# Global queries' scores for four head pairs in one pass of small pieces, the softmax division moved ahead of the values, and a new fixed order

## The chip, the cores and the metric

The kernel runs on one core of a Trainium2 chip. The metric is the device time of one execution in microseconds (us), as the median of several runs; lower is better. A core has five engines that run their own instruction streams and wait for each other by semaphores: TensorE (PE, matmuls), VectorE (DVE), ScalarE (ACT), GpSimd (POOL) and SyncE (SP, which here issues all DMAs).

## The reference

Attention with 32 global and 512 local tokens per head (8 batches, 8 heads, 64 numbers a head), then a gated product with two weight pairs. All inputs of the attention are float32, the weights float64; the output is float32.

```python
k_all, v_all = concat([k_g, k_l]), concat([v_g, v_l])
out_g = softmax(scale * q_g @ k_all.T) @ v_all            # 32 global queries see all 544 keys
s_ll  = where(abs(i - j) <= 32, scale * q_l @ k_l.T, -1e9) # local queries: a band
out_l = softmax(concat([scale * q_l @ k_g.T, s_ll])) @ concat([v_g, v_l])
x = concat([out_g, out_l]).transpose(...).reshape(8 * 544, 512)
out = ((x @ w1) * (x @ w2)) @ w3 @ w_out                   # 512 -> 1024 -> 1024 -> 512
```

Each softmax divides by its sum plus 1e-9.

## The kernel before

The work goes by pairs of heads, 32 pairs, four to a batch. Heads of a pair lie on partitions 0 to 63 and 64 to 127.

**A local pair.** Keys (tile `kr`, 128 x 544) and queries are loaded, keys are spread into `KT` so that each block of 32 queries finds its 128 keys in one stretch. `scores` (L412) makes 32 small float32 matmuls, each with 64 rows and 32 columns of weights and 128 moving columns, into the PSUM tile `s`. `minus_max` (L417, DVE) adds the mask and takes the minimum, `exps` (L423, ACT) makes the exponentials in place in `P` and their sums, `inverse` (L427, L428) the reciprocals. `turn` (L449, L452, DVE) transposes `P` by blocks into `TT` and `PT`, eight `move` steps (L466, L464) bring the blocks that belong to neighbours to their partitions, on whichever engine the plan names. `values` (L477 to L489) makes the products with the values into PSUM tile `av`, for the local queries and, from `TGr` and `TGg`, for the global ones. DVE and ACT add the two halves into `u`. The division by the sums is made here: `inverse_out` stores the reciprocals to DRAM (`rd`), `inverse_in` loads them spread over 64 partitions (`R`), and `normalize` (L444) multiplies `u` in two halves. `convert` splits `u` into a high and a low part (tiles `x`) for the gated product. From pair 5 on, `values` of a pair and `scores` of the next stand together on PE.

**Global queries.** In batch 0, `g_scores` (L523) multiplies a pair's keys by `QG`, in which the two heads' queries stand on the diagonal, in float32, 128 rows and 512 and 32 columns. In later batches keys are split into `kph` and `kpl` (`prep_kp`), queries into a high and a low half of `QG` (`prep_qg`), and four matmuls of the faster type float32r make the sum; ACT copies one half (`g_half`, `cg`) and DVE adds it (`g_minus_max`, L540). Two pairs share a tile `Pg`. `g_exps`, `g_normalize` follow, then, for batch 0, transposes on PE (`g_transposes`, L558), later block transposes on DVE and a trip over DRAM (`g_turn`, `g_out`, `g_in`, L576 to L589) into `TGr`.

**Weights.** Float64 words are loaded (`raw`, 512 KB each, three buffers), DVE and ACT make float32 of them (`unit`, L671 to L675). `fold` (L751) multiplies w3 by w_out on PE, eight tiles of 512 columns (`w`) with eight float32 products each, two PSUM banks. w1 and w2 (`w12`, eight numbers, four early in 512 KB pieces, four later in 256 KB pieces named `w12s`) are split into high and low parts.

**The gated product.** `first` (L617 to L619, tiles `ap`, `bp`) makes x @ w1 and x @ w2 in three float32r products, `gate_*` multiply and split, `second` (L649 to L651, `acc`) multiplies by the folded weights. It runs over two halves of each batch, four quarters a half, two w12 numbers a quarter.

**The order.** All steps are listed with what they wait for; `PLAN` holds, for every step, its place and its engine, and the program issues each engine's instructions in just this order. Each engine works strictly in its order. Tiles that are reused form rings: `pu` is the ring of two PSUM buffers (two banks each) that `s`, `av`, `sg` and `tg` share.

Of the kernel before, what the change touches and what calls it, by code (L numbers as in the profile page):

```python
# [20 lines left out]
KD, KX = 544, 832  # L21
# [6 lines left out]
def i(ap):  # L28
# [3 lines left out]
NX, NO, NK, NQ, MA = (5, 6), 3, 3, 3, 4  # L32
# [3 lines left out]
    kph=647, kpl=(726, 1374), qgh=298, qgl=(250, 461), kx=(440, 750, 1500), mmax=371, exps=500, inv=350, mul=(420, 740),  # L36
    turn=(1520, 790), move=(420, 420, 500, 560), cb=(590, 600), cu=(230, 200), sum=650, joing=500, xh=405, xl=(411, 740),
    cg=610, mg=790, eg=840, ng=820, wg=(683, 292), ga=588, gb=691, gh=620,
    gl=(691, 1295), out=587, shift=(434, 295), scale=(680, 440), merge=(676, 424), w12h=(676, 423),
    w12l=((691, 1300), (420, 752)), w34h=587, w34l=681, gscores=505,  # L40
    gtrans=465, gturn=1010, first=1372, second=1382, fold=860,
    scores=1290, values=2240, both=3110, gscores32=930,
# [3 lines left out]
FRONT = (("s", 0), ("sg", 0), ("sg", 1), ("s", 1), ("tg", 0))  # L46
# [3 lines left out]
IDLE = {None: ((0, 128, 256), (0, 64, 256), (64, 128, 256), (0, 64, 256), (64, 128, 256))}  # L50
# [12 lines left out]
    ('w3', 0, 0), ('wo', 0, 0), ('w3', 1, 0), ('wo', 1, 0), ('wo', 2, 0), ('wo', 3, 0), ('w3', 0, 1), ('wo', 4, 0),  # L63
    ('w3', 1, 1), ('wo', 5, 0), ('wo', 6, 0), ('wo', 7, 0), *[('w3', t, e) for t in range(2, 8) for e in range(2)],
    *[('w12', m, e) for m in range(MA) for e in range(2)],
)

# [3 lines left out]
    1V 632S 0V 2843V 3V 633S 8S 634D 677S 635D 329S 374S 10A 12S 636P 645D 637D 372P 638A 646A 152S 5V 647D 678S 648A  # L71
    649D 639D 16S 679A 641D 640A 643D 722S 651D 328S 642A 652A 375P 4V 9D 373D 11D 644A 376D 14A 650A 767S 20S 680A 7V
    377A 656D 681P 378D 379P 657D 380A 690D 663S 13D 682D 381D 684D 18A 692D 661A 15D 694D 660S 686D 382S 724A 696D
    687A 664V 658V 665D 659V 24S 695A 17D 662V 21D 723S 688D 683A 685A 22A 725A 383P 23D 812S 666P 689A 248P 697A 26A
    19D 691A 653D 384D 693A 6V 667A 28S 668A 25D 30A 27D 701D 702D 249P 710A 394A 669D 654S 386P 698D 726P 32S 154A
    258P 29D 2V 331S 706S 31D 703D 727D 707V 709A 735D 259P 705A 704D 387D 729D 737D 332V 334V 708V 731D 260P 769A 736A
    711P 158S 36S 34A 728A 388A 261P 250P 739D 251P 153D 732A 33D 741D 38A 35D 742A 40S 655S 37D 733D 39D 740A 730A 42A
    712A 44S 395D 389D 770A 713A 41D 333V 48S 768S 714D 43D 45D 738A 46A 335D 390P 252P 52S 47D 734A 385S 56S 391A 50A
    262P 396P 253P 747D 392A 49D 51D 397A 54A 263P 746D 670V 814A 771P 254P 671V 53D 60S 753A 264P 699S 55D 856S 748A
    780D 751V 755A 750A 674V 255P 398D 754A 749D 752V 772D 672A 64S 57D 256A 58A 773A 257D 774D 265P 59D 756P 782D 781A  # L80
    675A 62A 61D 68S 268P 63D 776D 700S 66A 269P 266D 72S 164S 70A 65D 270P 784D 400A 271P 67D 272P 778D 273P 743D 69D
    785A 267D 274P 278P 74A 275P 159D 779A 716D 279P 76S 786D 777A 71D 401D 676V 402P 280P 276D 775A 73D 75D 281P 673D
# [24 lines left out]
    1035V 899V 2120P 992P 441D 896D 978A 2131P 2132P 2127A 2133P 2134P 966S 442S 993D 1001D 979A 1003D 941D 995D 1002A
    996A 2135A 1005D 1006A 997D 999D 1007D 980D 445V 967S 939A 1004A 2128D 446D 1008A 1078V 998A 2136D 443S 994A 1000A
# [121 lines left out]
def band_attention_glu_kernel(  # L230
# [78 lines left out]
    def fresh(what, b):  # L309
# [899 lines left out]
```

## Time and profile before

| | |
|---|---|
| median of 3 runs | 772.17 us (771.96 to 774.92) |
| profiled execution: time | 772.31 us |
| profiled execution: span, first to last instruction | 770.6 us |
| mean granted TensorE clock | 0.989 |
| busy in the span: PE, DVE, ACT, POOL | 98%, 58%, 48%, 14% |
| HBM read and written | 61.57 MB, 12.94 MB |

Times are us from the start of the span. A row of the timeline has start, duration, engine, line, operation, tiles and shapes; "x8" says that eight records were merged into the row. A float32 matmul leaves two records. Matmul rows overlap, so what one costs is read from its start to the next row's start. Idle time stands in brackets with what ended it.

### The profile page before, as it was taken

To read this page: it belongs to the slowest core of one execution; us is meant where nothing else is said; L and a number is where in the kernel's file an instruction comes from. 1 tells how busy PE (TensorE), PEld (TensorE's weight loads), DVE (VectorE), ACT (ScalarE), POOL (GpSimd) and SP (SyncE) were. 2 spreads that over 40 slices of the span, in tenths; PEclk is the share of its full clock that TensorE was granted. 3 is DMA by queue.
4 is the path that set the end of the run, shared out by engine and by line. 5 is a ranking of instruction groups with operands and counts; after the bars stand their busy time and mean duration, and the time that the engine had idled before them with its cause. 6 is when DMAs were issued, how large, how long until landed. Compare 5 with 4: busy or idle time off the path is not lost.

```text
span 770.6 us, 22271 instructions
## 1 busy us (share of the span) xinstructions
PE 757.7 (98%) x9098; PEld 667.4 (87%) x9098; DVE 444.2 (58%) x1331; ACT 366.9 (48%) x1081; POOL 104.2 (14%) x194
## 2 busy tenths in 40 slices
PE   6999999999999999999999999999999999999998
PEld 4554589899999999999999999999999999999997
DVE  5889888565555647374666665665647474412121
ACT  4767777454444545354544455455446453312111
POOL 4110223434220001000001111010001001000000
PEclk7899999999999999999999999999999999999999
DMA  8887875223172313223232423241312121100000
GB/s 256 235 273 249 254 198 173 74 67 102 32 227 77 108 53 93 77 70 96 77 98 86 103 79 102 60 131 60 90 56 84 50 62 47 45 1 28 2 28 27
DMA packets 58301, 77.64 MB, mean 101 GB/s; under 512 B 19192, under 2 KB 28632, under 8 KB 58200
## 3 DMA queue, kind: packets, MB, share of 16 engines
q1 hardware_dynamic: 58200, 76.23, 33.3%
q8 instruction: 71, 1.16, 0.6%
q14 instruction: 30, 0.25, 0.1%
HBM read 61.57 MB, written 12.94 MB: 97 GB/s over the span
## 4 chain that ended last, share of the span: by engine, by line
PE 89%; DMA 4%; DVE 3%; ACT 2%; issue 1%; SPq 0%; POOL 0%; DVEq 0%; ACTq 0%
PE bp L617 8%; PE ap L617 8%; PE acc L649 8%; PE acc L651 8%; PE acc L650 8%; PE ap L618 8%; PE bp L618 8%; PE ap L619 8%; PE bp L619 8%; PE s L412 4%; PE av L477 4%; DMA raw_w<-in_w_t_dram 3%; PE sg L523 2%; PE w L751 2%; PE av L486 2%; PE av L482 2%
## 5 line engine op out<-in xcount | busy, mean ns | idle before, releaser
L617 PE MATMUL bp<-x,w12h 128*128 128x256 f32 x544 | 153.3, 282 | 0.2 <-issue 0.2
L617 PE MATMUL ap<-x,w12h 128*128 128x256 f32 x544 | 153.0, 281 | 0.3 <-ACT x L373 0.2
L618 PE MATMUL bp<-x,w12h 128*128 128x256 f32 x544 | 150.8, 277 | 0.6 <-issue 0.6
L618 PE MATMUL ap<-x,w12h 128*128 128x256 f32 x544 | 150.9, 277 | 0.2 <-DVE x L376 0.2
L619 PE MATMUL bp<-x,w12l 128*128 128x256 f32 x544 | 150.5, 277 | 0.0
L619 PE MATMUL ap<-x,w12l 128*128 128x256 f32 x544 | 150.5, 277 | 0.0
L423 ACT ACTIVATE P<-P,small 128x128 f32<-128x128 f32 x256 | 101.4, 397 | 34.5 <-DVE small L417 33.4
L417 DVE CUSTOM_DVE_ANT_0 P<-s,cs 128x128 f32<-128x128 f32 x256 | 68.0, 283 | 67.9 <-PE s L412 65.6
L617 PEld LDWEIGHTS ap<-x,w12h 128*128 128x128 f32 x544 | 102.1, 188 | 4.6 <-issue 1.6
L617 PEld LDWEIGHTS bp<-x,w12h 128*128 128x128 f32 x544 | 102.1, 188 | 4.5 <-issue 2.4
L618 PEld LDWEIGHTS bp<-x,w12h 128*128 128x128 f32 x544 | 102.4, 188 | 3.0 <-issue 1.3
L618 PEld LDWEIGHTS ap<-x,w12h 128*128 128x128 f32 x544 | 102.4, 188 | 2.5 <-DVE x L376 0.4
L619 PEld LDWEIGHTS ap<-x,w12l 128*128 128x128 f32 x544 | 102.2, 188 | 0.0
L619 PEld LDWEIGHTS bp<-x,w12l 128*128 128x128 f32 x544 | 102.2, 188 | 0.0
L751 PE MATMUL w<-wo,w3f 128*128 128x512 f32 x128 | 59.1, 609 | 0.1
L423 ACT ACTIVATION_READ_ACCUMULATOR P<-P,small 128x1 f32 x256 | 48.1, 188 | 0.0
L751 PEld LDWEIGHTS w<-wo,w3f 128*128 128x128 f32 x128 | 23.6, 193 | 26.8 <-issue 24.1
L466 ACT COPY PT<-TT 32x256 f32<-32x256 f32 (+1 forms) x101 | 39.1, 387 | 14.1 <-DVE TT L449 12.4
L373 ACT COPY u<-av 128x512 f32<-128x512 f32 (+1 forms) x40 | 19.1, 489 | 51.4 <-PE av L489 51.3
L449 DVE STREAM_TRANSPOSE TT<-P 128x1024 f32<-128x1024 f32 x32 | 38.9, 1217 | 1.9 <-ACT P L423 1.8
L412 PE MATMUL s<-KT,qp 64*32 64x128 f32 x2048 | 38.6, 281 | 1.0 <-POOL KT L318 0.6
L477 PEld LDWEIGHTS av<-PT,vr 64*64 64x64 f32 x1024 | 28.7, 135 | 10.9 <-issue 8.1
(789 smaller groups left out, 1430.9 us busy)
## 6 DMA issues: line engine op xcount, KB each, us to landing
raw_w<-in_w_t_dram SPq DMA_DIRECT2D x24, 512.0 KB, 5.8
kq<-in_kp_t_dram SPq DMA_DIRECT2D x32, 272.0 KB, 3.2
out_dram<-o_None SPq DMA_DIRECT2D x33, 256.0 KB, 2.6
qp<-in_q_t_dram SPq DMA_DIRECT2D x32, 256.0 KB, 3.2
vr<-in_v_t_dram SPq DMA_DIRECT2D x32, 256.0 KB, 3.7
R<-rd SPq DMA_DIRECT2D x64, 128.0 KB, 3.1
raw_wo<-in_wo_t_dram SPq DMA_DIRECT2D x8, 512.0 KB, 5.9
raw_w12s<-in_w_t_dram SPq DMA_DIRECT2D x16, 256.0 KB, 3.5
```

The source lines that it names most:

```text
L412: nc.tensor.matmul(st[32 * a : 32 * a + 32, x, 128 * e : 128 * e + 128], q[r, 128 * e + 32 * a : 128 * e + 32 * a + 32], k[r, o : o + 128] ...
L417: nc.vector.tensor_tensor_reduce(Ps[m % 2][:, x, e], T["s", m][:, x, 128 * e : 128 * e + 128], masks[e], -0.125, 3.0e38, ALU.add, ALU.min, ...
L423: nc.scalar.activation(p, p, AF.Exp, bias=T["mn", n][:, e : e + 1], scale=-1.0, accum_out=T["sm", m][:, x, e : e + 1])
L466: (nc.scalar.copy if eng is nc.scalar else eng.tensor_copy)(dst, src)
L477: nc.tensor.matmul(av[c, y, 128 * k + 32 * s0 : 128 * k + 32 * s1], V[r, x, k], PT[r, s0:s1, x, k], start=(k == 0), stop=False, **go)
L617: nc.tensor.matmul(d, wh[:, k, c, :], x[:, 0, 0:w], start=(k == m % 2 == 0), stop=False, skip_group_check=True)
L618: nc.tensor.matmul(d, wh[:, k, c, :], x[:, 1, 0:w], start=False, stop=False, skip_group_check=True)
L619: nc.tensor.matmul(d, wl[:, k, c, :], x[:, 0, 0:w], start=False, stop=(k == 3), skip_group_check=True)
L649: nc.tensor.matmul(a, gh[:, m % 2, sl], wh[:, c], start=(m == 0), stop=False, **part)
L650: nc.tensor.matmul(a, gh[:, m % 2, sl], wl[:, c], start=False, stop=False, **part)
L651: nc.tensor.matmul(a, gl[:, m % 2, sl], wh[:, c], start=False, stop=(m in (5, 7)), **part)
L751: nc.tensor.matmul(T["w34", t], T["w3f", t, j // 4][:, j % 4], T["wo"][:, j], start=(j == 0), stop=(j == 7))
```

## The change

The scores of a batch's global queries are made in one step, `g_scores(b)`: for each head a matmul of 64 rows by 32 columns in float32, four pairs on the four column groups, two heads on the two row groups, once over 512 and once over 32 key columns, into two `pu` buffers. The splits `kph`, `kpl`, the tile `QG`, the copy `cg` and the transposes on PE are gone; all batches take the way over DRAM into `TGr`. `Pg` now holds one head of each of the four pairs, so `values` takes the two heads from two tiles. The division by the sums is made in `P`, before `turn`, by one multiplication; `rd`, `R` and the two multiplications of `u` are gone. Folds use four PSUM banks (`acc` twice, and those of `ap` and `bp`), weights are fetched in another order, every fourth raw piece goes to a fourth buffer (that of `VG1`), key tiles get five buffers, and 11 idle products stand at the start instead of five. `PLAN` is another table throughout.

```diff
-NX, NO, NK, NQ, MA = (5, 6), 3, 3, 3, 4
+NX, NO, NK, NQ, MA = (5, 6), 3, 5, 3, 4
...
-FRONT = (("s", 0), ("sg", 0), ("sg", 1), ("s", 1), ("tg", 0))
+FRONT = (("s", 0), ("s", 1), ("sg", 0), ("sgk", 0))
-IDLE = {None: ((0, 128, 256), (0, 64, 256), (64, 128, 256), (0, 64, 256), (64, 128, 256))}
+IDLE = {None: ((0, 128, 256),) * 11}
...
-    ('w3', 0, 0), ('wo', 0, 0), ('w3', 1, 0), ('wo', 1, 0), ('wo', 2, 0), ('wo', 3, 0), ('w3', 0, 1), ('wo', 4, 0),
...
+    *[(k, a, 0) for a in range(4) for k in ("w3", "wo")], *[(k, a, e) for a in range(4) for k, a, e in (("w3", a, 1), ("wo", a + 4, 0))],
+    *[("w3", t, e) for t in range(4, 8) for e in range(2)], *[("w12", m, e) for m in range(MA) for e in range(2)],
...
+RAW = ((0, "raw", 3), (0, "raw", 3), (0, "raw", 3), (1, "VG1", 1))
+BANKS = ("acc", "acc", "a", "b", "a", "b", "acc", "acc")
...
 PLAN = """
-    1V 632S 0V 2843V 3V 633S 8S 634D 677S 635D 329S 374S 10A 12S 636P 645D 637D 372P 638A 646A 152S 5V 647D 678S 648A
...
-    def normalize(m, e, eng):
-        x = T["u", m][:, 32 + 256 * e : 288 + 256 * e].rearrange("r (a p) -> r a p", a=2)
-        inv = T["R", m].rearrange("r (p a) -> r a p", a=4)[:, 2 * e : 2 * e + 2]
-        eng.tensor_mul(x, x, inv)
+    def normalize(m, eng):
+        p = Ps[m % 2][:].rearrange("p x e k -> p (x e) k")
+        eng.tensor_mul(p, p, view(T.pop(("sm", m)), 0, [1, 8], [0, 128]))
...
-                nc.tensor.matmul(av[c, y, o : o + 32], V[r, x, k], TGr[r, 2 * (m % 2) + x, 32 * k : 32 * k + 32], start=False, stop=False, **go)
+                nc.tensor.matmul(av[c, y, o : o + 32], V[r, x, k], T["TG", x][r, p, 32 * k : 32 * k + 32], start=False, stop=False, **go)
...
+    def g_scores(b):
+
+        qg = T["qgr", b]
+        sg = T["sg", b] = [ps_1.tile([128, 2, 512], F32, tag="pu", name=f"sg{e}_{b}", bufs=2) for e in range(2)]
+        for e, c in enumerate((slice(0, 512), slice(512, S))):
+            for p in range(NP):
+                for x in range(2):
+                    r = slice(64 * x, 64 * x + 64)
+                    nc.tensor.matmul(sg[e][32 * p : 32 * p + 32, x, 0 : c.stop - c.start], qg[r, p], T["k2", NP * b + p][r, c],
+                                     start=True, stop=True, skip_group_check=True)
+
+    def g_minus_max(b, x):
+        g = 2 * b + x
+        Pg = T["Pg", g] = p1e.tile([128, S], F32, tag="Pg", name=f"Pg{g}", bufs=2)
+        mg = T["mg", g] = minima()[:, 8 + 3 * x : 11 + 3 * x]
+        for e, c in enumerate((slice(0, 512), slice(512, S))):
+            w = c.stop - c.start
+            nc.vector.tensor_tensor_reduce(Pg[:, c], T["sg", b][e][:, x, 0:w], cs[:, 300:301].to_broadcast([128, w]), -0.125, 3.0e38,
+                                           ALU.add, ALU.min, mg[:, e : e + 1])
+        nc.vector.tensor_tensor(mg[:, 0:1], mg[:, 0:1], mg[:, 1:2], ALU.min)
...
+            pool, tag, n = RAW[ORDER.index((kind, a, e)) % 4]
+            raw = (p1v if pool else P["early"]).tile([128, 512, 2], I32, tag=tag, name=name, bufs=n)
...
-            T["w34", t] = ps_acc.tile([128, 512], F32, tag="acc", name=f"w34_{t}")
+            tag = BANKS[t]
+            T["w34", t] = (ps_acc if tag == "acc" else ps_1).tile([128, 512], F32, tag=tag, name=f"w34_{t}")
```

On **PE at the start** (numbers behind a tile's name count its uses; `w34_0` is the first folded tile, `s0` the first local pair, `sg0` the first global one, `kq0` its keys), before:

```order
L412 MATMUL s0_181<-KT0_91,qp0_165 32x128 x32
L523 MATMUL sg0_217<-kq0_129,QG0_127 128x512
L523 MATMUL sg0_217<-kq0_129,QG0_127 128x32
L523 MATMUL sg1_246<-kq1_170,QG0_127 128x512
L523 MATMUL sg1_246<-kq1_170,QG0_127 128x32
L412 MATMUL s1_268<-KT1_92,qp1_226 32x128 x32
L558 MATMUL tg0_304<-cs_90,Pg0_251 128x128 x4
L559 MATMUL tg0_304<-cs_90,Pg0_251 32x128
```

and now:

```order
L318 MATMUL idle0_119<-TT_95 128x256 x11
L675 MATMUL w34_0_193<-wo_116,w3f0_0_177 128x512
L377 MATMUL s0_203<-KT0_91,qp0_185 32x128 x32
L675 MATMUL w34_0_193<-wo_116,w3f0_0_177 128x512
L675 MATMUL w34_1_252<-wo_116,w3f1_0_200 128x512
L377 MATMUL s1_258<-KT1_92,qp1_195 32x128 x32
L675 MATMUL w34_1_252<-wo_116,w3f1_0_200 128x512
L675 MATMUL w34_0_193<-wo_116,w3f0_0_177 128x512
L675 MATMUL w34_2_307<-wo_116,w3f2_0_250 128x512 x2
L675 MATMUL w34_3_320<-wo_116,w3f3_0_316 128x512
L675 MATMUL w34_2_307<-wo_116,w3f2_0_250 128x512
L675 MATMUL w34_3_320<-wo_116,w3f3_0_316 128x512
```

Ten folds have moved ahead of the first global scores, which stood second; the next row is the new global pass of batch 0.

On **PE in batch 2** (`sg10` is the global scores of pair 10, `kph10` and `kpl10` its split keys; `kq8` to `kq11` the keys of the batch), before:

```order
L619 MATMUL ap1_0_0_2454<-x1_2_0_2408,w12l0_105 128x256
L523 MATMUL sg10_2464<-kph10_2403,QG1_473 128x512
L523 MATMUL sg10_2464<-kph10_2403,QG1_473 128x32
L523 MATMUL sg10_2464<-kpl10_2413,QG1_473 128x512
L523 MATMUL sg10_2464<-kpl10_2413,QG1_473 128x32
L617 MATMUL bp1_0_0_2473<-x1_0_0_1916,w12h0_105 128x256
```

and now:

```order
L573 MATMUL acc0_1_128_2087<-w34h1_660,gl__1971 128x512
L473 MATMUL sg0_2_2118<-kq8_1325,qgr2_1850 32x512 x2
L473 MATMUL sg0_2_2118<-kq9_1733,qgr2_1850 32x512 x2
L473 MATMUL sg0_2_2118<-kq10_1965,qgr2_1850 32x512 x2
L473 MATMUL sg0_2_2118<-kq11_2060,qgr2_1850 32x512 x2
L473 MATMUL sg1_2_2119<-kq8_1325,qgr2_1850 32x32 x2
L473 MATMUL sg1_2_2119<-kq9_1733,qgr2_1850 32x32 x2
L473 MATMUL sg1_2_2119<-kq10_1965,qgr2_1850 32x32 x2
L473 MATMUL sg1_2_2119<-kq11_2060,qgr2_1850 32x32 x2
L539 MATMUL ap0_1_6_2155<-x0_0_1_804,w12h6_992 128x256
```

One step of sixteen matmuls for the whole batch, once a batch, stands where four matmuls for one pair stood, once a pair.

On **DVE around the turn of a pair** (`P0` the exponentials, `sums_101` their sums, `u7` the values of pair 7), before:

```order
L449 STREAM_TRANSPOSE TT_95<-P0_93 128x8x4x32
L452 STREAM_TRANSPOSE PT_96<-P0_93 128x8x2x32
L444 TENSOR_TENSOR u7_2329<-u7_2329,R7_2405 128x256
L466 COPY PT_96<-TT_95 32x256
L444 TENSOR_TENSOR u7_2329<-u7_2329,R7_2405 128x256
L427 TENSOR_SCALAR sums_101<-sums_101 128x8
L428 RECIPROCAL sums_101<-sums_101 128x8
```

and now, at another pair:

```order
L392 TENSOR_SCALAR sums_101<-sums_101 128x8
L393 RECIPROCAL sums_101<-sums_101 128x8
L398 TENSOR_TENSOR P0_93<-P0_93,sums_101 128x1024
L403 STREAM_TRANSPOSE TT_95<-P0_93 128x8x4x32
L406 STREAM_TRANSPOSE PT_96<-P0_93 128x8x2x32
L420 COPY PT_96<-TT_95 32x256 x2
```

The reciprocals stood behind the turn and the division behind the values; both now stand ahead of the turn.

## Rows read from the trace of the kernel before

**Rows 1.** Busy time by stretch: PE, PEld, DVE, ACT, POOL; then clock, DMA share, GB/s.

```profile
0.00:27.40 27.40, 20.72 (x243) 13.50 (x244) 17.66 (x66) 15.91 (x52) 8.58 (x29) 0.69 0.82 250
...
27.40:98.00 70.60, 69.61 (x606) 36.26 (x605) 60.92 (x162) 49.45 (x131) 12.76 (x21) 1.00 0.84 255
98.00:132.60 34.60, 34.17 (x491) 30.92 (x491) 29.34 (x84) 25.98 (x70) 10.30 (x16) 1.00 0.65 177
132.60:770.60 638.00, 633.18 (x7762) 586.75 (x7762) 336.31 (x1022) 275.51 (x829) 72.58 (x129) 1.00 0.25 73
```

**Rows 2.** Timeline of PE at the start.

```profile
24.67 2.92 PE L751 MATMUL w<-wo,w3f 128*128 128x512 f32 x4
27.43 1.16 PE L523 MATMUL sg<-kq,QG 128*128 128x512 f32 x4
28.52 1.16 PE L412 MATMUL s<-KT,qp 64*32 64x128 f32 x64
```

**Rows 3.** Timeline of PE among the folds.

```profile
38.08 0.63 PE L558 MATMUL tg<-cs,Pg 128*128 128x128 f32 x4 [0.89 <-DVE Pg L552]
...
40.53 0.62 PE L523 MATMUL sg<-kph,QG 128*128 128x512 f32 x2
...
41.34 1.96 PE L751 MATMUL w<-wo,w3f 128*128 128x512 f32 x4
...
58.21 0.81 PE L523 MATMUL sg<-kph,QG 128*128 128x512 f32 x2
...
59.21 19.13 PE L751 MATMUL w<-wo,w3f 128*128 128x512 f32 x44
...
92.38 0.81 PE L523 MATMUL sg<-kph,QG 128*128 128x512 f32 x2
...
93.38 1.10 PE L751 MATMUL w<-wo,w3f 128*128 128x512 f32 x2
```

**Rows 4.** Timeline of PE, values and scores between larger products.

```profile
108.38 0.28 PE L619 MATMUL bp<-x,w12l 128*128 128x256 f32 x1
108.58 1.09 PE L477 MATMUL av<-PT,vr 64*64 64x96 f32 x29
...
110.67 1.16 PE L412 MATMUL s<-KT,qp 64*32 64x128 f32 x64
111.76 0.50 PE L649 MATMUL acc<-w34h,gh__1291 128*128 128x512 f32 x1
112.10 0.39 PE L650 MATMUL acc<-w34l,gh__1291 128*128 128x512 f32 x1
```

**Rows 5.** Timeline of PE at one pair's global scores.

```profile
121.46 0.41 PE L523 MATMUL sg<-kph,QG 128*128 128x512 f32 x2
...
122.06 0.47 PE L649 MATMUL acc<-w34h,gh__1508 128*128 128x512 f32 x1
122.37 0.39 PE L650 MATMUL acc<-w34l,gh__1508 128*128 128x512 f32 x1
```

**Rows 6.** Timeline of DVE and PE where the last w12 is made and read.

```profile
131.05 0.43 DVE L376 TENSOR_TENSOR w12l<-raw_w12s,w12h 128x256 fp32r<-128x256 f32 x1 [0.17 <-ACT w12h L373]
...
132.48 0.38 PE L617 MATMUL ap<-x,w12h 128*128 128x256 f32 x1
```

**Rows 7.** Timeline of one pair: turn, last move, values.

```profile
175.45 1.24 DVE L449 STREAM_TRANSPOSE TT<-P 128x1024 f32<-128x1024 f32 x1
...
182.44 0.39 POOL L466 COPY PT<-TT 32x256 f32<-32x256 f32 x1
...
184.98 1.05 PE L477 MATMUL av<-PT,vr 64*64 64x96 f32 x32
```

**Rows 8.** Groups of DVE by line and form, and the page's DMA issues.

```profile
L540 DVE CUSTOM_DVE_ANT_0 Pg<-sg,cg 64x544 f32<-64x544 f32 x28 | 20.0, 715 | 16.8 <-ACT cg L528 16.5
...
L758 DVE TENSOR_TENSOR w34l<-w,w34h 128x512 fp32r<-128x512 f32 x8 | 5.5, 686 | 0.7 <-ACT w34h L373 0.6
...
kq<-in_kp_t_dram SPq DMA_DIRECT2D x32, 272.0 KB, 3.2
```

More of the change, by code (lines that the diff above doesn't have):

```diff
@@ L811, in tile_orders @@
         for k in FRONT:
-            take("pu", 2, k, ("sp", k[1]) if k[0] == "s" else k)
-        for b in range(2):
-            take("QG", 1, ("QG", b), ("clear", "QG", b))
+            take("pu", 2, k, ({"s": "sp", "sgk": "sg"}.get(k[0], k[0]), k[1]))
         for m in range(NH // 2):
@@ L829, in values_need @@
     def values_need(m):
-        tg = [("gw", m // 2, e) for e in range(2)] if m < NP else [("tgi", m // 2)]
-        return [("move", m, c) for c in range(8)] + [("load", "v", m), ("load", "vg", m // NP), *tg]
+        b = m // NP
+        return [("move", m, c) for c in range(8)] + [("load", "v", m), ("load", "vg", b), ("tgi", 2 * b), ("tgi", 2 * b + 1)]
     def values_read(m):
-        read(products(m), ("TT", m), ("PT", m), ("vr", m), ("VG", m // NP), ("TG", m // 2))
+        read(products(m), ("TT", m), ("PT", m), ("vr", m), ("VG", m // NP), ("TG0", m // NP), ("TG1", m // NP))
     def head(m):
@@ L872, in head @@
         for x in range(2):
-            add(("turn", m, x), only("DVE", COST["turn"][x]), t + x, [("exps", n, e) for n in (2 * m, 2 * m + 1) for e in range(4)] + [("clear", "PT", 0)], turn, m, x)
+            add(("turn", m, x), only("DVE", COST["turn"][x]), t + x, [("norm", m), ("clear", "PT", 0)], turn, m, x)
             read(("turn", m, x), ("P", m))
@@ new lines, in global_batch @@
+    def global_batch(b):
+        t = base(8 * b) if b else 0.0
+        ms = range(NP * b, NP * b + NP)
+        me = ("sg", b)
+        add(me, only("PE", COST["gscores"]), t - 30.0, [("load", "qg", b), *[("load", "k2", m) for m in ms]], g_scores, b)
+        read(me, ("qg", b), *[("k2", m, "r") for m in ms])
+        for x in range(2):
+            g = 2 * b + x
+            take("Pg", 2, ("Pg", g), ("mg", b, x))
+            add(("mg", b, x), only("DVE", COST["mg"]), t - 29.0 + x, [me, ("load", "cs"), *[("mg", b, 0)] * x], g_minus_max, b, x)
+            read(("mg", b, x), ("sg", b), ("sgk", b))
+            add(("eg", g), only("ACT", COST["eg"]), t - 27.0 + x, [("mg", b, x)], g_exps, g)
+            add(("ng", g), only("DVE", COST["ng"], True), t - 26.0 + x, [("eg", g)], g_normalize, g)
+            take("tgs", 1, ("tgs", g), ("tg", g))
+            add(("tg", g), only("DVE", COST["gturn"]), t - 25.0 + x, [("ng", g)], g_turn, g)
+            read(("tg", g), ("Pg", g))
+            add(("tgo", g), dma(380), t - 24.0 + x, [("tg", g)], g_out, g, nbytes=278528)
+            read(("tgo", g), ("tgs", g))
+            take(f"TG{x}", 1, (f"TG{x}", b), ("tgi", g))
+            add(("tgi", g), dma(450, 450, 450, 450, 450), t - 20.0, [("tgo", g), ("clear", "TGg", 0)], g_in, g, nbytes=278528)
@@ L1064, in weight @@
         me = [("unit", *u, j) for j in range(6)]
-        tag = "o" if small else "raw"
-        take(tag, NO if small else 3, ("raw", *u), ("fetch", *u))
+        tag = "o" if small else "raw" if ORDER.index(u) % 4 < 3 else "rawv"
+        take(tag, dict(o=NO, raw=3, rawv=1)[tag], ("raw", *u), ("fetch", *u))
         add(("fetch", *u), dma(390), t - 12.0, (), fetch, *u, nbytes=(262144 if small else 524288))
@@ L1086, in product @@
         due = [max(due["w3", t, j // 4], due["wo", j, 0]) + FD for j in range(8)]
-        take("acc", 2, ("w34", t), ("fold", t, 0))
+        take(BANKS[t], 2 if BANKS[t] == "acc" else 1, ("w34", t), ("fold", t, 0))
         for j in range(8):
@@ L1118, in band_attention_glu_kernel @@
         batch(b)
+    for b in range(B):
+        global_batch(b)
     for m in range(NH // 2):
-        global_pair(m)
         pair_values(m)
```

477 lines of the change are left out of this document (160 added, 317 removed).

## Prediction

> **What bounds the kernel now.** I read the page's head first, then the busy time by stretch, then TensorE's own timeline where the change touches it, and last the rows of the engines that feed it. The span is 770.6 us, as the table has it. TensorE (PE) is busy for 69.61 of the 70.6 us from 27.4 to 98, for 34.17 of the next 34.6 and for 633.18 of the last 638; the vector engine (DVE) is at 86%, 85% and 53% there [rows 1]. [...] A busy matmul row alone proves little, since rows overlap, so I checked starts: 44 records of the folds w follow each other in 19.13 us, 0.43 each [rows 3], with no gap. So from 27.4 us on the time is the sum of PE's work in program order, and a change gains what it takes out of that sum, unless something else becomes late.
>
> I cut the run at a **mark**: the first matmul on w12 number 7, the last weight to be made, at 132.48 [rows 6]. Behind it lie 638.1 us of the span. Both programs have the same matmuls of the kinds ap, bp and acc on each side of the same mark (counted from the order), so only the attention's own PE work differs.
>
> **The change, step by step.**
>
> *Old global scores, behind batch 0.* One pair takes from 121.46 to 122.06, 0.60 us, and the first acc behind it 0.31 instead of 0.23 [rows 5]: 0.68. Among the folds it is dearer: 0.81 at 40.53 and 1.00 at 58.21 and 92.38 [rows 3]. Of the 28 pairs, 24 lie behind the mark: 24 x 0.68 = 16.3 us. The other four are 0.81 + 1.00 + 1.00 + 0.60 = 3.4.
>
> *Old global scores of batch 0.* One pair at full clock takes from 27.43 to 28.52, 1.09 us [rows 2]; four are 4.4 us of full-clock work. Two transposes tg of about 0.6 [rows 3] go too: 1.2.
>
> *New scores.* Eight passes, each of 8 pieces of 512 columns and 8 of 32, on 64 rows x 32 columns of the array. No row shows this shape. The nearest is s: 32 pieces of 128 columns on the same eight sub-arrays, each with moving data of its own, in 1.09 us [rows 4]. By column count one full-array pass over 544 columns took 1.09, so 128 cost a quarter, about 0.26, and 32 in a row would be 8.2: the sub-arrays overlap 7.5 times. Sixteen pieces in a row would be 8 x 1.09 = 8.7; divided by 7.5 that is 1.16. Bounds: 1.09 (eight at once) and 8.7 (none). I take 1.15, by the s row, which has the same tiles and the same source pattern.
>
> *The trip between shapes.* The av at 108.58 starts 0.20 behind its predecessor where ap and bp follow each other at 0.11, and the first acc behind s takes 0.34, not 0.23 [rows 4]: 0.2 for a trip into small tiles and out. So a new pass costs 1.35. [...]
>
> *What stands on the other side of the mark.* The new order reaches the mark with 6 s and 5 av instead of 7 and 6. One av and s with its trip is 111.76 - 108.58 + 0.2 = 3.4 us [rows 4]; it moves behind the mark.
>
> Behind the mark: -16.3 + 6 x 1.35 + 3.4 = **-4.8**. Ahead of it: -3.4 (av, s) - 3.4 - 4.4 - 1.2 + 2 x 1.35 = **-9.7**.
>
> *The front.* The old one has by 27.43 done two s, three sg, a tg, an av and two folds, at full clock 2.2 + 3.3 + 0.6 + 2.1 + 1.7 = 9.9 us, so 17.5 are lost to the start. The new one puts folds first and then waits for the fourth key tile. Ahead of that tile on the SP queue are 9 raw weights, 4 kq, 2 qp and a qgr, 6.4 MB; at the 250 GB/s of the first stretch [rows 1] that is 25.7 us, or 28.7 if the 3 us of a first landing [rows 8] come on top. Ten folds (8.7) and two s lie ahead of it: 14.8 to 17.8 lost. Then the folds follow the weights for some 25 us and can lose another 2. I take no difference, with -3 to +3. The eleven idle products run while PE would wait for data; if data came sooner, they would cost what is left of them.
>
> *The division.* It moves from the finished values (two multiplications of 128x256 behind av) to one of 128x1024 between the sums and the turn, all 32 on DVE by the order. A tensor_tensor of 128x512 takes 0.69 [rows 8], so this one takes at most 1.37; I take 1.3. It now stands in the chain that av waits for. In the pair shown the turn starts at 175.45, the last move ends at 182.83 and av starts at 184.98 [rows 7]: 2.1 us are free, and the moves are not hurried. So nothing in the sum; with the cover gone it is 1.3 a pair.
>
> *What goes beside PE.* Key splits, copies of half scores, the trip of the sums over DRAM with its broadcast, and two multiplications a pair leave DVE, ACT, POOL and the SP queue; the queue no longer stands at a store of sums with loads behind it. PE waits for none of these behind the mark, so they gain nothing there. Ahead of the mark they matter: the last w12l ends at 131.48 and its matmul starts at 132.48 [rows 6]. The weights are **one microsecond** ahead of PE. If PE is to be there 9.7 us sooner, DVE, ACT and the loads must be as well. On DVE eight reductions of 0.72 [rows 8], four key splits and a whole pair's reductions and turn fall away ahead of that point, four double reductions, five divisions and three more turns come, in all some 7 us less. A fourth raw slot lets loads run further ahead.
>
> **Sum.** 770.6 - 9.7 - 4.8 = 756.1 of span. The profiled execution took 772.31 with 1.7 outside its span, and the median of the runs is 772.17, so the two are one scale: **758 us**, 1.8% less.
>
> **Rivals.**
> 1. *The weights set the mark.* They are as late as before, the mark stays at 132.5, and only the 4.8 behind it are kept: 758 + 9.7 = 767.5. For it: the one microsecond above, and DVE at 85%. Against it: 7 us less on DVE and the larger prefetch. Halfway it is 762, inside my range. 0.14.
> 2. *The division is late.* If the moves end after av's turn, each of the 27 pairs behind the mark loses up to 1.3: +35, 793, slower than before. It decides from 0.67 a pair (18 us over my sum is +0.5%). Against it: 2.1 us of slack in the pair shown, and DVE at 53%. 0.06.
> 3. *Both score banks at once.* A pass fills both buffers that s and av share; they come free after four reductions, two of about 0.7 and two short ones, some 2.2 us. Seven passes behind the first, fully exposed: +15, 773, no change. [...] Against it here: in the order 36 matmuls of first products and 12 of acc, some 7 us, lie between a late pass and the next av. 0.04.
> 4. *The pieces run one after another*, so the change doesn't do what it says: 8 x (8.7 - 1.15) = +60, 818. Only a difference between s and these pieces could do it, and I see none in tiles or operands. 0.03.
>
> **How the numbers follow.** My forecast gets 0.69. 0.04 is left for better than the range, where the front gains more. Low end: 758 less 3 (front), 1.6 (no trip), 0.5 (passes at their lower bound) and 1.4 (PE's idle from 27.4 to the mark [rows 1]): 751. High end: 768, which takes in rival 1; rivals 2 to 4 (0.13) and the 0.04 stay out. A measurement of this kernel can tell about 0.5% (3.9 us) from no change, so faster is below 768.3: 0.69 + 0.04 and most of rival 1 (0.08), 0.81. Same: the rest of rival 1 and most of rival 3, 0.10. Slower: rivals 2 and 4, 0.09.
>
> **What would show it.** Right: sg passes near 1.2 us from start to next start; first matmul on w12 number 7 near 123; PE without idle behind it; 633 us from there to the end. Wrong at the new scores: a pass of several us. Wrong ahead of the mark: PE idle or w12l ending right at the matmul that reads it. Wrong at the division: PE idle at av, released by a move PT<-TT, with the multiplication of P in the chain of waits. Wrong at the banks: s or av idle, released by the reduction of Pg.

## The result and the profile after

The changed kernel takes 762.03 us (median of 4 runs, 760.83 to 762.56) against 773.1 us (771.96 to 774.92) for the kernel before in the same job: ratio 0.9852, 95% interval 0.9827 to 0.9878. The forecast of 758 us was 4 us too low; its range of 751 to 768 holds the result. The profiled execution took 760.83 us with a span of 759.1, so 1.7 us lie outside the span, as before.

Busy time by stretch, kernel after (columns as in [rows 1]). The cuts are at 27.4 us, at the start of the scores of pair 3 (67.5), at 92 us, shortly behind the first products on w12 (89.6), and at the mark:

```profile
0.00:27.40 27.40, 22.57 (x205) 13.02 (x206) 14.31 (x59) 12.39 (x28) 5.40 (x24) 0.94 0.85 288
27.40:67.50 40.10, 38.80 (x310) 18.32 (x308) 36.34 (x90) 27.06 (x78) 4.52 (x9) 1.00 0.90 290
67.50:92.00 24.50, 20.67 (x257) 12.51 (x257) 24.16 (x58) 19.09 (x50) 9.53 (x11) 0.93 0.63 199
92.00:125.55 33.55, 33.06 (x457) 29.93 (x456) 28.08 (x96) 22.64 (x68) 9.71 (x14) 1.00 0.69 199
125.55:759.10 633.55, 629.12 (x8007) 578.23 (x8005) 341.14 (x1057) 244.94 (x779) 48.22 (x89) 1.00 0.20 61
```

The last row is the forecast's stretch behind the mark: TensorE (PE) is busy for 629.12 of 633.55 us. The third row is the one to note. There PE is idle for 3.8 us of 24.5, the vector engine (DVE) works 99% of the time, and the DMA share, 0.90 in the row above, is 0.63.

The mark in the timeline of PE, and the last split of w12 on DVE (answers to [rows 6]):

```profile
125.32 0.39 PE L573 MATMUL acc<-w34h,gl__1592 128*128 128x512 f32 x1
125.55 0.28 PE L539 MATMUL ap<-x,w12h 128*128 128x256 f32 x1
```
```profile
125.75 0.89 DVE L359 TENSOR_TENSOR w12l<-raw_w12s,w12h 128x256 fp32r<-128x256 f32 x1
```

The mark is at 125.55, where 122.8 was forecast (132.48 less 9.7). Behind it lie 633.55 us, where 638.1 - 4.8 = 633.3 was forecast. So the miss lies ahead of the mark. (The last split starts behind the mark: the number comes in pieces, and the last piece is read 1.3 us behind the mark, at 126.82, 0.2 us after it is done.)

A global pass between products in the timeline of PE (answers to [rows 5]):

```profile
156.16 0.39 PE L573 MATMUL acc<-w34h,gl__1971 128*128 128x512 f32 x1
156.48 1.15 PE L473 MATMUL sg<-kq,qgr 64*32 64x512 f32 x32
157.56 0.38 PE L539 MATMUL ap<-x,w12h 128*128 128x256 f32 x1
157.78 0.28 PE L540 MATMUL ap<-x,w12h 128*128 128x256 f32 x1
```

From start to next start the pass takes 1.08 us (1.15 forecast). The acc ahead of it is followed after 0.32 and not 0.23, and the first ap after 0.22 and not 0.115: 0.2 for the trip. So a pass costs 1.28 (1.35 forecast).

PE at the start (answers to [rows 2]), and where it waits later:

```profile
11.73 1.22 PE L675 MATMUL w<-wo,w3f 128*128 128x512 f32 x2 [3.26 <-DVE wo L597]
12.87 1.96 PE L377 MATMUL s<-KT,qp 64*32 64x128 f32 x64
14.76 2.60 PE L675 MATMUL w<-wo,w3f 128*128 128x512 f32 x4
17.29 1.16 PE L377 MATMUL s<-KT,qp 64*32 64x128 f32 x64
...
25.23 1.15 PE L473 MATMUL sg<-kq,qgr 64*32 64x512 f32 x32
...
43.67 7.99 PE L675 MATMUL w<-wo,w3f 128*128 128x512 f32 x18 [1.24 <-DVE wo L597]
...
83.14 1.09 PE L431 MATMUL av<-PT,vr 64*64 64x96 f32 x29 [1.41 <-DVE raw_w L593]
...
87.71 1.96 PE L377 MATMUL s<-KT,qp 64*32 64x128 f32 x64 [2.42 <-ACT w12h L356]
89.60 0.58 PE L539 MATMUL ap<-x,w12h 128*128 128x256 f32 x1
...
91.21 0.28 PE L540 MATMUL ap<-x,w12h 128*128 128x256 f32 x1
...
98.74 0.39 PE L540 MATMUL ap<-x,w12h 128*128 128x256 f32 x1 [0.48 <-DVE x L359]
```

The work before 25.23 is ten folds and two s, 10.9 us at full clock: 14.3 us are lost there, against 17.5 before. Behind it the kernel before had PE busy for 69.61 of 70.6 us [rows 1]; now PE waits 1.24, 1.41, 2.42 and 0.48 us. After the third wait the scores of pair 4 take 1.89 and not 1.09 from start to next start, and the next seven products 1.61 and not 0.81: the granted clock is 0.51 from 87.7 to 89.6 us, 0.52 from there to 91.2 and 1.00 from there to 95. The longer steps are 1.6 us in all.

The profile ascribes the third wait to a conversion of w12 on ACT, which the scores do not read. The last of the steps ahead of it whose result they do read, as far as the rows show, is a copy of keys on DVE, done at 87.45 (runs 11 and 12 name it for the same wait). Ahead of it DVE has a division and a step on raw weights that takes 1.79 us:

```profile
83.03 1.22 DVE L398 TENSOR_TENSOR P<-P,sums 128x1024 f32<-128x1024 f32 x1
84.17 1.79 DVE L597 SCALAR_TENSOR_TENSOR raw_w<-raw_w 128x512 int32<-128x512 int32 x1
...
87.28 0.17 DVE L338 COPY KT<-kq 128x32 f32<-128x32 f32 x1
```

The division: one row of its group on the page, and one pair behind the mark (answers to [rows 7]) from the timelines of DVE, ACT and PE.

```profile
L398 DVE TENSOR_TENSOR P<-P,sums 128x1024 f32<-128x1024 f32 x32 | 39.2, 1225 | 0.6
```
```profile
173.79 1.34 DVE L398 TENSOR_TENSOR P<-P,sums 128x1024 f32<-128x1024 f32 x1
175.17 1.25 DVE L403 STREAM_TRANSPOSE TT<-P 128x1024 f32<-128x1024 f32 x1
...
178.36 1.26 ACT L420 COPY PT<-TT 32x256 f32<-32x256 f32 x3
...
181.76 1.05 PE L431 MATMUL av<-PT,vr 64*64 64x96 f32 x32
```

A division takes 1.225 us (1.3 forecast). In this pair the last move ends at 179.62 and av starts at 181.76: 2.1 us are free, as in the pair that the prediction shows.

### The profile page after: what moved, and what is told of

Same layout as the page of the kernel before. It is cut to its first block, busy times and chain, and to the rows that moved or that the text cites. A ratio compares the mean times of both kernels' runs of the same rounds, so it can differ in the third digit from the quotient of the medians.

```text
span 759.1 us, 22082 instructions
## 1 busy us (share of the span) xinstructions
PE 744.2 (98%) x9228; PEld 652.0 (86%) x9228; DVE 444.0 (58%) x1351; ACT 326.1 (43%) x1000; POOL 77.4 (10%) x145
## 4 chain that ended last, share of the span: by engine, by line
PE 83%; DVE 2%; ACT 1%; DMA 1%; issue 0%; POOL 0%; SPq 0%; DVEq 0%; ACTq 0%; POOLq 0%
PE bp L539 8%; PE ap L539 8%; PE acc L571 8%; PE acc L573 8%; PE acc L572 8%; PE ap L540 8%; PE bp L541 8%; PE bp L540 8%; PE ap L541 8%; PE s L377 4%; PE av L431 3%; PE av L440 2%; PE av L436 2%; PE sg L473 1%; DMA raw_w12s<-in_w_t_dram 1%; ACT P L388 0%
## 5 line engine op out<-in xcount | busy, mean ns | idle before, releaser
L382 DVE CUSTOM_DVE_ANT_0 P<-s,cs 128x128 f32<-128x128 f32 x256 | 64.7, 285 | 68.0 <-PE s L377 68.0
L356 ACT COPY u<-av 128x512 f32<-128x512 f32 (+1 forms) x58 | 22.6, 399 | 63.5 <-PE av L442 61.6
L398 DVE TENSOR_TENSOR P<-P,sums 128x1024 f32<-128x1024 f32 x32 | 39.2, 1225 | 0.6
```

Of the source, the lines that this page charges most:

```text
L382: nc.vector.tensor_tensor_reduce(Ps[m % 2][:, x, e], T["s", m][:, x, 128 * e : 128 * e + 128], masks[e], -0.125, 3.0e38, ALU.add, ALU.min, ...
L398: eng.tensor_mul(p, p, view(T.pop(("sm", m)), 0, [1, 8], [0, 128]))
```

## The experiments

My theory after reading this: behind the mark the time is PE's sum, and the new scores cost what their rows show. Ahead of the mark the preparation of the weights decides, so less work on PE there is worth less than its length. The rivals: the passes cost more than their rows; the division is late; the clock alone explains the miss; the loads alone explain it.

The landmarks are from one profiled execution of each run, which lies up to 3.0 us off the run's median (run 6) and 1.9 above it in run 1: the starts of the scores of pairs 3 and 4, the mark, and what of the span lies behind it. Ratios are against the kernel before, timed in the same job. Runs 0, 1, 2 and 4 shared one job, 3, 5, 7 and 9 another, 6, 11 and 12 a third, 13 was alone (the numbers 8 and 10 are not used); medians are compared within a job where one serves as the measure.

| run | median us | ratio, 95% interval | pair 3 | pair 4 | mark | behind |
|---|---|---|---|---|---|---|
| first profile of after | 762.03 | 0.9827 to 0.9878 | 67.50 | 87.71 | 125.55 | 633.6 |
| 0, after again | 762.22 | 0.9858 to 0.9900 | 67.63 | 87.97 | 125.69 | 634.1 |
| 1, pass twice | 769.22 | 0.9945 to 0.9974 | 70.40 | 90.48 | 130.19 | 639.1 |
| 7, before, half scores | 764.23 | 0.9870 to 0.9913 | | | 131.01 | 630.5 |
| 3, division twice behind | 769.58 | 0.9949 to 0.9979 | 67.96 | 88.26 | 125.55 | 642.0 |
| 2, no division in front | 758.35 | 0.9806 to 0.9848 | 68.15 | 85.41 | 122.69 | 634.1 |
| 4, five idle products | 763.91 | 0.9875 to 0.9910 | 67.97 | 88.16 | 127.77 | 633.8 |
| 5, unread products in the gap | 762.04 | 0.9850 to 0.9895 | 67.30 | 87.61 | 125.78 | 633.3 |
| 9, one division later | 760.57 | 0.9829 to 0.9866 | 66.68 | 85.24 | 124.16 | 633.6 |
| 11, 9 and keys earlier | 762.61 | 0.9847 to 0.9895 | 67.22 | 85.59 | 125.96 | 632.8 |
| 12, 11 and four buffers | 762.11 | 0.9845 to 0.9890 | 69.38 | 87.84 | 129.93 | 632.5 |
| 13, 9 and unread products | 762.87 | 0.9864 to 0.9903 | 68.31 | 87.85 | 126.39 | 634.8 |
| 6, divisions on GpSimd | 764.39 | 0.9885 to 0.9933 | 70.55 | 92.71 | 130.94 | 634.7 |

**Run 0: the kernel after, unchanged.** 

> The changed kernel as it is, timed beside the next three on one chip, so that they can be compared with it. Expected 762 us, the first matmul on w12 number 7 (the mark) near 125.5 us, as in the first profile of it.

As expected; it is the measure for runs 1, 2 and 4. It and the other runs that change nothing behind the mark (first profile, 2, 4, 5, 6, 9, 11, 13) have 632.8 to 634.8 us there, so differences in that column are good to about 2 us.

**Run 1: the price of a new pass.**

```diff
-            for p in range(NP):
+            for p, _ in [(p, n) for n in range(2) for p in range(NP)]:
```

> Every piece of the global scores is made twice (same result), eight passes more in all, seven of them behind the profile's first 30 us and six behind the mark. My theory (a pass costs what its row shows, 1.08 us, pieces on eight sub-arrays at once, and TensorE's sum is the time behind the mark): +6 x 0.97 to 1.08 = 5.8 to 6.5 us behind the mark, and 0 to 2.2 ahead of it, so 768 to 771. Rival, pieces one after another: +60. Rival, the trip between tile shapes and the emptied banks are the cost and the pieces are nearly free: under +3.

Measured: +7.0 us. A doubled pass in this run:

```profile
161.00 2.28 PE L473 MATMUL sg<-kq,qgr 64*32 64x512 f32 x64
163.21 0.39 PE L539 MATMUL ap<-x,w12h 128*128 128x256 f32 x1
```

It takes 2.21 us where one takes 1.08, so the second costs 1.13. Behind the mark six more passes cost 5.0 us, 0.83 each, a little under my lower bound; the column's 2 us of spread cover the difference. Ahead of it two cost 4.5 in this profiled execution, more than their own length, but that execution is 1.9 us above the median; PE's waits for weights among the folds, which vary from execution to execution, are part of it (6.1 us against 5.1 in run 0). The pieces do run at the same time; the rivals (+60, and under +3) fall.

**Run 7: the price of the old scores.** In the old kernel:

```diff
+        ks = ks[-1:]
         for j, k in enumerate(ks):
```

> The old kernel with two of the four matmuls of every later pair's global scores left out (the products with the high half of the keys), everything else in place; the global rows are then wrong. It prices the old scores by themselves. My theory (behind the mark the time is TensorE's sum; two matmuls of 0.60 us for four are 0.30): 24 x 0.30 = 7.2 us behind the mark and up to 4 x 0.45 = 1.8 ahead of it, 763 to 765 against 772. Rival (something else than TensorE's sum bounds the old kernel): under 2 us less.

Measured: 772.54 to 764.23. Behind the mark 630.5 us are left of 638.1: 7.6 less for 24 halves, 0.32 each. Ahead of the mark it is 1.5 (1.8 at most). What is left of a pair's scores:

```profile
120.16 0.41 PE L524 MATMUL sg<-kpl,QG 128*128 128x512 f32 x2
120.42 0.48 PE L650 MATMUL acc<-w34h,gh__1502 128*128 128x512 f32 x1
120.74 0.40 PE L651 MATMUL acc<-w34l,gh__1502 128*128 128x512 f32 x1
```

It takes 0.26, and the first acc behind it 0.32 and not 0.23: 0.35 in all. With the 0.32 that went, a pair is 0.67, where I had 0.68. PE's work taken from the old kernel came off its time nearly in full, ahead of the mark too.

**Run 3: the cover of the division.**

```diff
-        eng.tensor_mul(p, p, view(T.pop(("sm", m)), 0, [1, 8], [0, 128]))
+        inv = view(T.pop(("sm", m)), 0, [1, 8], [0, 128])
+        for _ in range(1 + (m > 4)):
+            eng.tensor_mul(p, p, inv)
```

> The multiplication of P is made twice for pairs 5 to 31, all behind the mark (P is then divided twice). 27 x 1.22 us more on VectorE, in the chain between the sums and the values of each pair. My theory (the division is covered there by some 2 us of slack): 0 to +1 us. Rival (the division bounds, its cover is gone): up to +33 us; between them, a gain would be had from taking it off the chain.

Measured: 642.0 us behind the mark against 633.6 to 634.1, so some 8 us of the 33 added come through: neither of the two forecasts. The four longest waits of PE behind the mark in this run (us in total, times, longest):

```profile
PE acc L575 <- DVE gl__4749 L359: 1.5, 1, 1.5
PE bp L541 <- DVE small L494: 1.2, 1, 1.2
PE av L433 <- DVE PT L422: 0.9, 1, 0.9
PE av L433 <- ACT PT L422: 0.6, 1, 0.6
```

They are single places, not one for each pair. All waits listed there add up to 6.7 us, against 1.2 in the kernel after; the remaining 2.4 to 2.9 us show as longer busy time of PE and are not placed. Of the four, one is held by a split of the gated product (gl), one by the normalization of a batch's global rows (L494), two by moves. In the kernel after I compared the start of av with the end of the last move ahead of it at 28 pairs from 119 us on: 21 have 3.3 us or more between them, three 1.7 to 2.7, and four under 0.8. So one division is covered nearly everywhere, and a second is not at a few tight places. What no division at all behind the mark would give was not run.

**Run 2: less on DVE ahead of the mark.**

```diff
+        if m > 4:
+            eng.tensor_mul(p, p, inv)
```

> The multiplication of P by the reciprocals is left out for pairs 0 to 4, all ahead of the mark; the output of these pairs is then not divided. It takes 5 x 1.22 = 6.1 us off VectorE before the mark, 3.7 of it before 85 us, where VectorE is 97% busy. My theory (VectorE's preparation of weights sets the time up to the mark): the mark comes 2 to 4 us earlier, about 123, and the time is 758 to 760. Rival, the loads of the weights set it: the mark moves by less than 0.5 and VectorE shows idle time ended by DMA instead. Rival, the fixed order of TensorE alone: no change.

Measured: 3.9 us less, the mark at 122.69, 3.0 earlier. Where it came from tells more. Three of the five divisions (at 41.79, 51.91 and 64.94 in the kernel after) end before the scores of pair 3 start, and those do not start earlier (68.15 against 67.63). From there to pair 4 it is 17.3 us and not 20.3. The waits of DVE before pair 3, first the kernel after, then this run:

```profile
DVE raw_w L593 <- DMA raw_w<-in_w_t_dram: 2.5, 2, 1.5
```
```profile
DVE raw_w L595 <- DMA raw_w<-in_w_t_dram: 4.8, 3, 2.3
```

Of the 3.7 us saved on DVE, 2.3 turn into more waiting for loads. PE still waits 1.1 us for weights in that stretch, against 1.24. No more than that was to be won there, since PE is busy for 38.80 of the 40.10 us. So there are two limits in turn: up to some 67 us PE's own work, with the loads (DMA share 0.90, 290 GB/s) behind the little that it waits, then to 92 us DVE. This run's own row of that second stretch shows it:

```profile
68.10:92.00 23.90, 22.30 (x335) 13.97 (x336) 22.59 (x68) 19.69 (x55) 9.03 (x12) 1.00 0.71 230
```

Without the division of pair 3 in this stretch and that of pair 2 just ahead of it PE is busy for 22.30 of 23.90 us, and the granted clock is 1.00 in place of 0.93. My theory had only DVE. (Four of the five divisions, 4.9 us, lie ahead of 85 us, not the 3.7 that I expected.)

**Run 4: the idle products at the start.**

```diff
-IDLE = {None: ((0, 128, 256),) * 11}
+IDLE = {None: ((0, 128, 256), (0, 64, 256), (64, 128, 256), (0, 64, 256), (64, 128, 256))}
```

> The five idle products of the old kernel stand at the start in place of eleven. [...] Rival, the clock at the start carries the gain ahead of the mark in full: +2 to +3 us.

Measured: 763.91 us, 1.7 above run 0, where I had put 762 to 763 by way of a later start; the loss is not made at the start. The same rows as above in this run:

```profile
12.14 2.04 PE L675 MATMUL w<-wo,w3f 128*128 128x512 f32 x2 [7.72 <-DVE wo L597]
14.12 1.73 PE L377 MATMUL s<-KT,qp 64*32 64x128 f32 x64
15.78 1.98 PE L675 MATMUL w<-wo,w3f 128*128 128x512 f32 x4
17.70 1.16 PE L377 MATMUL s<-KT,qp 64*32 64x128 f32 x64
```

From the first fold to the second s it is 5.56 us with five idle products and 17.29 - 11.73 = 5.56 with eleven: they gain nothing there. Pair 4 starts 0.2 later than in run 0, and the rest is lost behind it, where the clock stayed low longer (granted 0.50 to 91.9 us and 0.66 from there to 95, where run 0 has 0.74 from 89.9 to 91.9 and then 1.00). The intervals of the two runs overlap; I don't count it as an effect of the edit.

**Run 5: the clock at 88 us.** Behind the values of pair 2:

```diff
+            if k == ("av", 2):
+                z = ps_1.tile([128, 512], F32, tag="b", name="gap")
+                for _ in range(5):
+                    nc.tensor.matmul(z[:, 0:256], cs[:, 0:128], cs[:, 0:256], start=True, stop=True)
```

> Same result. Five products that nobody reads (128 columns of weights, 256 columns moved) stand between the values of pair 2 and the scores of pair 4, where TensorE waits 2.4 to 3.1 us. They keep it busy about 2.2 us. If the clock falls because TensorE idles there, the scores of pair 4 take 1.09 us again in place of 1.96 and the first products behind them 0.115 each: 1.5 to 1.6 us earlier at 92 us, and 760.6 if nothing else is late. Rival, the last pieces of w12 hold the mark by then (they are 0.2 us ahead of TensorE): the 1.6 us turn into a wait before the mark and the time stays at 762.

Measured: no change (762.04), though the clock did what I expected:

```profile
87.61 1.19 PE L377 MATMUL s<-KT,qp 64*32 64x128 f32 x64
88.73 0.38 PE L539 MATMUL ap<-x,w12h 128*128 128x256 f32 x1
```

The scores take 1.12 and not 1.9 us, and the mean granted clock of the execution is 0.998, against 0.996 in the first profile of the kernel after. By the pass of batch 1 (96.14 against 96.78) 0.6 of it are left, by the mark nothing. It went into waits of 0.25 us for moves of pair 3 and 0.34 for an x, and 0.67 that the profile ascribes to nothing. Run 3 says the same: up to pair 4 its program is that of the kernel after, and there the clock did not fall behind a wait as long.

```profile
88.26 1.15 PE L377 MATMUL s<-KT,qp 64*32 64x128 f32 x64 [2.62 <-ACT w12h L356]
```

Its pair 4 starts 0.3 to 0.6 us later, the granted clock is 1.00, and its mark is at 125.55 all the same. So the clock alone is not the cause: what PE regains there the next late piece takes.

**Runs 9, 11, 12 and 13: a better order?** Run 9 moves one word of the table (626D, the division of pair 3) from ahead of 147D to ahead of 628D:

```diff
-    146A 323P 142A 687S 314A 145D 626D 147D 648A 595P 324A 647S 148A 315D 596A 143V 325D 649D 149D 557V 449S 597A 598D
-    154A 600A 155D 160A 650P 601D 628D 4V 728S 627D 1803P 730A 769S 166A 161V 167V 630D 602A 1805P 659D 636A 632V 651D
+    146A 323P 142A 687S 314A 145D 147D 648A 595P 324A 647S 148A 315D 596A 143V 325D 649D 149D 557V 449S 597A 598D
+    154A 600A 155D 160A 650P 601D 626D 628D 4V 728S 627D 1803P 730A 769S 166A 161V 167V 630D 602A 1805P 659D 636A 632V 651D
```

> Same result. The division of pair 3 stands in VectorE's order behind the last early weights and directly ahead of its turn, and not ahead of them (there it took 83.0 to 84.2 us). [...] Rival, the division does not matter where it stands: no change.

Run 11 also puts 648A ahead of 314A and 649D ahead of 315D (the keys of pair 4):

> Same result. The run with pair 3's division later (760.6), and also the spreading of pair 4's keys on ScalarE and VectorE ahead of the splits of the last folds, since it was the last thing that the scores of pair 4 waited for. They start 0.6 to 1.2 us earlier. My theory (one order on VectorE, what is moved ahead of one reader makes another late): the next wait is at the values of pair 3, whose moves then end no sooner; mark 0 to 0.7 us earlier, 759.9 to 760.6. Rival, the wait for pair 4's keys was the last obstacle: the whole 1.3 us, 759.3.

Run 12 is run 11 with four output buffers:

```diff
-NX, NO, NK, NQ, MA = (5, 6), 3, 5, 3, 4
+NX, NO, NK, NQ, MA = (5, 6), 4, 5, 3, 4
```

> The kernel before this one with four buffers in place of three in the ring that the late w12 pieces and the outputs share. The fetches of these pieces stood blocked on the load queue for 5.3 us behind a full ring at 115 us. If the ring holds the mark, the last pieces land some 3 us earlier and the mark comes earlier by what TensorE has ready: up to 0.5 us. If TensorE's earlier waits hold it: no change against the kernel before this one.

Run 13 is run 9 with three of run 5's unread products:

> Same result. The division of pair 3 later, as in the run of 760.6, and three products that nobody reads between the values of pair 2 and the scores of pair 4, where that run still waited 1.3 us. In that run two of four executions had a mean granted clock of 1.000 and two 0.996; the unread products should hold the clock in all of them: 759.5 to 760.6, mark near 124. Rival (nothing left to win at that place, the rest is spread): 760.6 to 761, as without them.

Measured: run 9 has 760.57, inside the 759.3 to 761 that I had put, and yet it shows little. Its pair 3 already started 0.8 to 1.0 us earlier than in the kernel after, ahead of the place of the edit, so only some 0.6 us of the mark's 1.4 to 1.5 can be the edit's; its interval overlaps that of run 0; and runs 11, 12 and 13, which contain its edit, are at 762.1 to 762.9. From pair 3 to pair 4 the edit does save 1.7 to 2.0 us in runs 9, 11 and 12 (18.4 to 18.6 us against 20.2 and 20.3). It is gone by the values of pair 3, whose turn now stands behind the division: run 11 waits 1.71 us there for a move. Run 11's earlier keys did not bring pair 4 forward (85.59 against 85.24), run 12's fourth buffer did not bring the mark forward (its profiled execution has a stop of 2.90 us besides, shown at the end), and in run 13 the granted clock was 1.00 behind the gap and the time did not fall. No version that makes all the divisions beats the changed kernel by more than its spread.

**Run 6: the divisions on GpSimd.** In the table 500D, 542D, 584D, 626D and 668D become 500V, 542V, 584V, 626V and 668V.

> Same result. The divisions of pairs 0 to 4 are made by GpSimd and not by VectorE, at the same places of the order. It takes the same 6.1 us off VectorE as leaving them out (which gave 3.9 us), and puts them on an engine that is idle for most of the first 100 us. In the profile of the changed kernel four of VectorE's steps on raw weights took 0.95 to 1.79 us in place of 0.42 or 0.68, each beside a multiplication or subtraction of GpSimd. If GpSimd's work holds VectorE up like that, and each division takes GpSimd some 2.5 us, most of the gain is given back and each pair's turn is 1.3 us later: 760 to 765. Rival, work on GpSimd is free: 758.4 to 759.

Measured: 764.39, as expected. That is some 2 us above the kernel after, but its interval overlaps that of run 0, so only this is sure: the gain of leaving the same five out, 3.9 us, is gone. GpSimd and DVE in this run:

```profile
50.47 1.90 POOL L398 TENSOR_TENSOR P<-P,sums 128x1024 f32<-128x1024 f32 x1 [3.90 <-DVE sums L393]
```
```profile
50.77 2.15 DVE L597 SCALAR_TENSOR_TENSOR w3f<-raw_w 128x512 int32<-128x512 int32 x1
```

The step on DVE, 0.68 us elsewhere, ends 0.55 us after the division on GpSimd does. DVE lost 1.5 us beside a division that would have cost it 1.2. Three more of the five divisions have a step of DVE beside them that took 1.13, 2.18 and 2.15 us and 0.42 to 0.43 elsewhere, so beside four of them DVE lost 5.7 us. No row shows what held these steps.

## Why the prediction was right or wrong

**What bounds the kernel** was right behind the mark: run 7 took 0.34 us a pair off PE's rows (0.60 to 0.26), 8.2 in all, and gained 7.6, and the changed kernel has 4.4 us without PE in 633.6.

**Old and new global scores** were right: 0.67 for 0.68 a pair (run 7), 1.28 for 1.35 a pass. With these the sum behind the mark is -24 x 0.67 + 6 x 1.28 + 3.4 = -5.0, with mine -4.8; measured -4.55, and the spread of 2 us can't tell the three apart. A trip between the shapes took 0.2 us in both kernels.

**The division** was right where it was counted, at nothing behind the mark, with two limits: the slack of 2.1 us that I took from one pair does not hold for every pair (run 3), and ahead of the mark it did cost. There it is 1.2 us a pair on the engine that sets the pace from 67 to 92 us. With the five front divisions left out (run 2) the time is 758.35 and the mark at 122.69, which are my 758 and 122.8: what they cost there is as large as the whole miss. That does not make them its only cause: no run freed as much of DVE's time there in another way. I had written the five divisions into DVE's balance (7 us less in all) and then not asked what the engine still had to do between two dates.

**What failed is the front term**, "I take no difference, with -3 to +3". By the prediction's prices PE's work ahead of the mark fell by 9.7 us, and the mark came 6.9 sooner (132.48 to 125.55), so 2.8 us more are lost there than before. That this lies inside the bound is luck: it has two parts of opposite sign, and each is outside what I had allowed for it. Up to the pass of batch 0 the loss fell from 17.5 to 14.3, just past the end of my bound. From there to the mark it rose by 6.0, where I had allowed 2: PE's idle time rose by 4.2 (5.6 us now, the waits of 1.24, 1.41, 2.42 and 0.48, against 1.4 before), and 1.6 are the low clock behind the third (0.51 and 0.52). No run took back the front's other changes (the order of the fetches, the fourth raw buffer, the four banks) one by one, so what each gave is open; the idle products gave nothing that run 4 can show.

**The reason** is the one that the prediction named as its first rival and held for unlikely: "If PE is to be there 9.7 us sooner, DVE, ACT and the loads must be as well." The mark came 6.9 sooner. Run 2 tells which: the loads for the little that PE waits up to some 67 us, then DVE; run 5 that the clock alone is not the cause. The 7 us that I had credited DVE with were 5 (107.9 us busy before 132.48; 102.9 before the mark now, 14.31 + 36.34 + 24.16 + 28.08). Part of the missing 2 is that steps on raw weights took longer: the 24 shifts of raw_w 0.53 us for 0.46 and the eight merges in place 0.83 for 0.69, the longest of each beside work on GpSimd as in run 6 (1.52 from 66.08 beside 1.31 from 66.00, and 1.79 from 84.17 beside 1.36 from 84.06).

**Rivals.** The first came in by three tenths (2.8 of 9.7 lost), and with both of its signs: PE idle, and the last split done at 126.64 for a read at 126.82. The second needed 0.67 a pair; nothing shows it. The third: no wait for a reduction of Pg is in the list. The fourth: 1.08 us, not 8.7. The sign and the size were right because the part that I could price from dense rows, -4.8 and most of -9.7, was most of the change.

## What to carry to other kernels

Where an engine was dense here, its removed work came off the time nearly in full (run 7: 8.2 us off PE's rows, 7.6 off the time); where it is fed, ask by which date each feeder is ready, stretch by stretch, since the limit changes hands (here PE itself with the loads close behind, then DVE) and part of a gain on one is given back to the next (run 2: 2.3 of 3.7 us). A rival that is half true belongs in the sum as a share, not only in the range. And compare landmarks ahead of the edited place before crediting an edit with a microsecond.

## What I had not expected of the hardware

In run 12 PE stood for 2.90 us in the middle of one step, with nothing in the profile to wait for:

```profile
87.84 0.70 PE L377 MATMUL s<-KT,qp 64*32 64x128 f32 x33 [1.28 <-DVE KT L338]
91.44 1.10 PE L377 MATMUL s<-KT,qp 64*32 64x128 f32 x31 [2.90 <-issue]
```

Runs 9 and 11 have a gap of 0.33 and 0.65 us at the same place, between the same two records. The DMA view lists queues of instructions beside those of data; over the whole run of the kernel after:

```profile
q1 hardware_dynamic: 44312, 68.32, 28.8%
q8 instruction: 72, 1.18, 0.6%
```

The columns are packets, MB and share. A packet of that queue appears in the half microsecond from 88.5 in run 12, from 84.5 in run 11 and from 83.5 in run 9, and PE goes on at 91.44, 86.94 and 86.27, 1.9 to 2.9 us after the packet. In run 12 the queue of data took 97.4% of the DMA engines from 84 to 88 us. In the kernel after such a packet falls between 84 and 85 us, where PE waits until 87.71 anyway, and no gap shows. That a late packet of instructions held PE is argued from these times alone: no row shows whose instructions a packet holds, and no run here moved it.
